# Wider unread streams, and a matrix inverse moved forward by a step, in a fused recurrence and expert kernel

## The chip, the cores and the metric

The kernel runs on one core of a Trainium2 chip. The metric is device time in microseconds from start to end of one launch. The engines are PE (TensorE: matrix products), DVE (VectorE), ACT (ScalarE), POOL (GpSimd) and SP (SyncE, which here does nothing but issue DMAs). Each works through its own instructions in order.

## What is computed

A linear recurrence with a 40x40 state for each of 32 heads (4 batches by 8), over 768 positions, then a layer of eight experts with one chosen for each token, then a dense layer with a squared ReLU.

```python
for t in range(S):                        # 768 positions, batch x heads = 32
    y[:, :, t] = np.einsum('bhd,bhde->bhe', rt, state)
    Sa = np.einsum('bhde,bhe->bhd', state, at)
    state_decay = state * wt[:, :, None, :] - np.einsum('bhd,bhe->bhde', Sa, bt)
    state = state_decay + np.einsum('bhd,bhe->bhde', vt, kt)
...
h = np.maximum(xc[mask] @ w1[e], 0.0)     # 3072 tokens, D 320, F 1024, 8 experts
y[mask] = gate_w[mask, None] * (h @ w2[e])
...
r = np.maximum(x @ w_in, 0.0); return (r * r) @ w_out      # 320 x 2048 x 320
```

## The kernel before

The recurrence is done in 24 **steps** of 32 positions; four steps are a **slab**, so a step is the first, second, third or fourth of its slab (`r = c%4`), and step numbers here count from 0. In a step each head needs the inverse of a 32x32 triangular matrix, which is made for a whole slab at once (128 matrices, one to a partition). The way of those matrices sets the order of much of the work around the change:

1. `L(c)` multiplies a chunk's operands, and its DVE part leaves the triangular table in `zs`; SP stores it to DRAM (`nt<-zs`, L154).
2. `tul(c)` loads it back with heads on partitions into `TU` (`tu<-nt`, L157): four loads a slab. In `run`, the first two are issued at the start of the slab before, the other two right behind their stores (`lst`).
3. `inv(sl)` inverts the two 16x16 halves on DVE: 14 pairs of a product (L177) and a sum (L179). At its end ACT and DVE write the off-diagonal part, transposed, into `TW`, and SP stores both to DRAM (`td<-tu`, `td<-tw`, L187). Before, about three fifths of its pieces come in the third step (places 12 to 32 of that step's table) and the rest in the fourth (places 0 to 8).
4. `ttfill(c,H)` loads one half (`H` 0 or 1, 16 heads each) of a step's matrices into `TT` and `SW` (L213, eight loads of 16 KB). It is issued right behind the stage V of the step before, since V is the last to read `TT`, which exists once.
5. `Pst` (L196) is the first product that reads them; `Qst` (L204) completes the inverse. `Pst` of the next step's half 0 is the last stage of a step (`P0+` in `ORD`).

The order of PE's stages is written out by hand (`ORD`, `ORD2` for third steps, `END`). Between the stages `pump` issues what stands in a table `sched` at places 0 to 32: pieces of the inverse, of decay factors, of routing and of weight conversion. All loads and stores named here share SP's queue, and an issue that must wait holds back what stands behind it.

Stages Z, U and S begin with **unread streams** (`keep`, L94): products whose result nobody reads, written to the unused end of the stage's PSUM bank. They multiply 128 columns of the identity by 256 (Z) or twice by 192 (U and S) bf16 columns of it. The stage V (L260) has none.

```python
ORD=('Z0 U1- V1- Q0 Y0- K1- T0 X U0 V0 S1- K0 R S0 P1 Z1 Y1- T1 Q1 L P0+').split()
```

After the recurrence come the experts and the dense layer (from about 646 us), which the change doesn't touch.

Of the kernel before, what the change touches and what calls it, by code (L numbers as in the profile page):

```python
# [12 lines left out]
BF16 = mybir.dt.bfloat16  # L13
# [7 lines left out]
class Attn:  # L21


    IB=3.4
    I2=(12, 32)
    I3=(0, 8)
    RT=(13, 18)
    RP=(0, 8)
    MP=(12, 26)
# [61 lines left out]
    def pair(s): return s.pp.tile([128,2,512],F32,tag='pp',name='pp')  # L91
    def keep(s,o):

        b=s.ident.bitcast(BF16); s.nc.tensor.matmul(o,b[:,0:128],b[:,0:o.shape[1]],start=True,stop=True)  # L94
    r=0
    def pump(s,n):
        while n>0 and s.fill: s.fill.pop(0)(); n-=1
# [137 lines left out]
            nc.scalar.copy(out=ys[64:128,16*k:16*k+16].rearrange('p (x i r) e -> p x i r e',i=2,r=2)[:,:,i],in_=src)  # L235
    def Zst(s,c,H):
        nc=s.nc; zs=s.g(s.ZS,c); m=s.M1; z=s.Z; pt=s.slot()
        s.keep(pt[:,256:512])
        for j in range(4):
            for i in range(4):  # L240
                h=16*H+4*i+j
                nc.tensor.matmul(pt[32*i:32*i+32,40*j:40*j+40],zs[:,h,:],m[:,h,0:40],start=True,stop=True)
        nc.scalar.activation(out=z[:,4*H:4*H+4,0:40],in_=pt[:,0:160].rearrange('p (g d) -> p g d',d=40),func=AF.Copy,scale=-1.0)
    def Ust(s,c,H):

        nc=s.nc; z=s.Z; tt=s.TT; pt=s.pair()
        for k in range(2): s.keep(pt[:,k,320:512])
        for ii in range(2):
            for j in range(4):
                for k in range(2):  # L250
                    i=2*k+ii; b=slice(64*k,64*k+64); n=160*ii+40*j
                    nc.tensor.matmul(pt[96:128,k,n:n+40],tt[b,4*H+j,32*i:32*i+32],z[b,4*H+j,0:40],start=True,stop=True)  # L252
        for k in range(2):
            nc.scalar.copy(out=s.VU[96:128,16*H:16*H+16].rearrange('p (k x) d -> p k (x d)',k=2)[:,k],in_=pt[96:128,k,0:320])
    def Vst(s,c,H):

        nc=s.nc; z=s.Z; tt=s.TT; ut=s.UT; pt=s.slot()
        for j in range(4):
            g=4*H+j; q=j//2; par=j%2
            nc.tensor.matmul(pt[64*par:64*par+64,128*q:128*q+128],z[:,g,:],tt[:,g,:],start=True,stop=True)  # L260
        nc.scalar.copy(out=ut.rearrange('p (H i q) t -> p H q i t',H=2,i=4)[:,H,:,:,32:64],
                       in_=pt[:,0:256].rearrange('p (q i t) -> p q i t',q=2,i=4))
    def Sst(s,c,H):
        nc=s.nc; ys=s.YS; m=s.VU; mn=s.M1; d=s.g(s.DL,c+1); pt=s.pair()
        for k in range(2): s.keep(pt[:,k,320:512])
        for n in range(8):
            for k in range(2):
                h=16*H+8*k+n
                nc.tensor.matmul(pt[64*k:64*k+40,k,40*n:40*n+40],ys[:,h,:],m[:,h,:],start=True,stop=True)  # L269
        for k in range(2):  # L270
            h=slice(16*H+8*k,16*H+8*k+8)
            nc.vector.tensor_tensor(out=mn[0:40,h,0:40],in0=pt[64*k:64*k+40,k,0:320].rearrange('p (x d) -> p x d',d=40),  # L272
                in1=d[:,h].unsqueeze(2).to_broadcast([40,8,40]),op=ALU.mult)
# [19 lines left out]
    def run(s, sink, more=None, before=None):  # L293
# [26 lines left out]
        for c in range(NC):  # L320
            sl=c//4; r=s.r=c%4; nx=sl+1<s.NS; last=c==NC-1; order=s.END if last else s.ORD2 if r==2 else s.ORD
            if before: before(c)
            sched=[[] for _ in range(NP+1)]
            def add(items,p0,p1):
                for i,f in enumerate(items): sched[p0+i*(p1-p0)//len(items)].append(f)
            def take(budget):
                o=[]
                while s.invq and budget>0: j,f=s.invq.pop(0); o.append(f); budget-=j
                return o
            at=lambda p,*f: sched[p].extend(f)  # L330
            xs=[]; Ls=[]

            if c==0:
                at(6,lambda: (s.tul(4),s.tul(5)),*s.decay(3))
                at(7,lambda: s.prod(6,(V,G,G))); at(9,lambda: s.prod(7,(V,G,G)))
                Ls+=[6,7]
            for P in (sl+1,sl+2):
                d=c-4*(P-2); A=2*P; B=A+1
                if P>=s.NS or P<2: continue
                if d==4: at(0,lambda A=A: (s.tul(2*A),s.tul(2*A+1)))  # L340
                if d==(0 if P>2 else 1): add(s.decay(A),0,14)
                if d==(1 if P>2 else 2): add(s.decay(B),0,12)
                for k in range(4):
                    if d==k+1: at(s.PP,lambda x=2*A+k,w=s.PA[k]: s.prod(x,eng(w)))
                    if d==min(k+2,4): Ls.append(2*A+k)
            if nx:
                if r==2: s.invq=s.inv(sl+1); add(take(s.IB),*s.I2)
                if r==3: add(take(99),*s.I3)
            add(late[0],*s.RP); add(late[1],*s.SC); late=([],[])
            if more:  # L350
                m0,m1=more(c); add(m0,4,NP); add(m1,s.MP[0],s.MP[1])
            if c>1:
                x,pre,post,sc=sink(c-2,s.XT) or ([],[],[],[])
                xs.append(x); add(pre,*((18,22) if last else s.RT)); late=(post,sc)
                if last: add(post+sc,22,30); late=([],[])
            if last:
                x,pre,post,sc=sink(c-1,s.XT) or ([],[],[],[])
                xs.append(x+pre+post+sc)
            pc=[0]
            def pump(n=1):  # L360
                for _ in range(n):
                    if pc[0]<=NP:
                        for f in sched[pc[0]]: f()
                    pc[0]+=1
            def lst(x):
                s.L(x)
                if x<4*sl+8: s.tul(x)
            for st in order:
                k=st[0]; H=int(st[1]) if st[1:] else 0; b=c-st.endswith('-')+st.endswith('+')
                if c==0 and st=='U0': s.turn_tt(); s.L(4); s.L(5); s.Pst(0,0); s.Pst(0,1); s.Qst(0,0); s.Qst(0,1)  # L370
                if b<0: continue
                if k=='Z': s.Zst(b,H); s.load_v(b+1,H)
                elif k=='Y': s.Y(b,H); s.load_y(b+1,H)
                elif k=='T': s.Stt(b,H)
                elif k=='U': s.Ust(b,H)
                elif k=='V':
                    s.Vst(b,H)
                    s.ttfill(b+1,H)
                elif k=='K':
                    s.KBt(b,H)  # L380
                    if H: s.load_k(b+8)
                elif k=='R':
                    hs=[(1,c)] if st=='R1' else [(1,c-1),(0,c)][c==0:]
                    s.RUV([H for H,b in hs])
                    for H,b in hs: s.load_r(b+1,H)
                elif k=='S': s.Sst(b,H); s.load_vu(b+1,H)
                elif k=='P' and b: s.Pst(b,H)
                elif k=='Q' and b: s.Qst(b,H)
                elif k=='X':
                    for f in xs.pop(0) if xs else (): f()  # L390
                elif k=='L':
                    for x in Ls[len(Ls)>1 and c>0:]: lst(x)
                pump(s.PW[k])
                if st=='T0' and c and len(Ls)>1: lst(Ls[0]); pump()
            while pc[0]<=NP: pump()
        x,pre,post,sc=sink(NC-1,s.XT)
# [409 lines left out]
def build(tc, ins, out):  # L806
    nc = tc.nc
    NC = 24
    NPC, NPD = 7, 7
    with ExitStack() as ctx, tc.manual_schedule():  # L810
# [4 lines left out]
        with ExitStack() as c2:  # L815
# [2 lines left out]
            fctx = ctx.enter_context(ExitStack())  # L818
            at = Attn(tc, ins, NC, c2, ident, c3, "right")
            rt = Route(tc, ins, ident, at.ps, cp, dr, at.cp)  # L820
            conv = cv.seq(0, NPC, 2) + cv.seq(NPC, NPD, 1) + cv.seq(NPD, 16, 0)
            NV = {16: 6, 17: 6, 18: 6, 20: 6, 21: 6, 22: 6, 23: 6}

# [60 lines left out]
```

## Time and profile before

| | us |
|---|---|
| median of 3 runs | 1178.79 (1176.95 to 1184.74) |
| profiled execution, its own time | 1181.23 |
| its span, first to last instruction | 1179.5 |
| PE busy with products | 989.7 |
| DVE busy | 610.5 |
| ACT busy | 485.5 |
| POOL busy | 294.2 |

The span is what the trace covers; what lies around it in the profiled execution is 1.7 us. Mean granted TensorE clock over the span: 0.835 of full speed; the clock has two levels, 1.2 GHz (0.50) and 2.4 GHz (1.00), so a mean between them tells how the time is shared out. A busy share is an average over stages with different limits, so it is read by stretch.

### The profile page before, as it was taken

To read this page: it belongs to the slowest core of one execution; us is meant where nothing else is said; L and a number is where in the kernel's file an instruction comes from. 1 tells how busy PE (TensorE), PEld (TensorE's weight loads), DVE (VectorE), ACT (ScalarE), POOL (GpSimd) and SP (SyncE) were. 2 spreads that over 40 slices of the span, in tenths; PEclk is the share of its full clock that TensorE was granted. 3 is DMA by queue.
4 is the path that set the end of the run, shared out by engine and by line. 5 is a ranking of instruction groups with operands and counts; after the bars stand their busy time and mean duration, and the time that the engine had idled before them with its cause. 6 is when DMAs were issued, how large, how long until landed. Compare 5 with 4: busy or idle time off the path is not lost.

```text
span 1179.5 us, 40064 instructions
## 1 busy us (share of the span) xinstructions
PE 989.7 (84%) x17280; PEld 902.3 (77%) x17280; DVE 610.5 (52%) x1132; ACT 485.5 (41%) x1115; POOL 294.2 (25%) x293
## 2 busy tenths in 40 slices
PE   2196877997898988788785789887999999999997
PEld 2175666775777777576575689886999999999997
DVE  8983463455546334452425698784644444444331
ACT  6343443444444355344332555542433333333331
POOL 6222211321311314332424523225211111110000
PEclk9996776677768568676755799998999999999999
DMA  6656555455445444447532898873000010100000
GB/s 186 169 158 192 146 129 147 122 131 144 120 124 139 113 117 124 127 143 188 138 86 80 239 273 257 284 232 109 22 28 28 28 28 27 29 29 24 13 12 20
DMA packets 165306, 138.68 MB, mean 118 GB/s; under 512 B 109887, under 2 KB 139237, under 8 KB 165121
## 3 DMA queue, kind: packets, MB, share of 16 engines
q1 hardware_dynamic: 160865, 124.97, 38.4%
q0 software_dynamic: 4256, 11.06, 3.0%
q8 instruction: 138, 2.26, 0.8%
q14 instruction: 47, 0.39, 0.1%
HBM read 107.65 MB, written 32.85 MB: 119 GB/s over the span
## 4 chain that ended last, share of the span: by engine, by line
PE 62%; DMA 16%; DVE 9%; issue 6%; SPq 5%; ACT 2%; POOL 0%; ACTq 0%; POOLq 0%; DVEq 0%
PE fps L585 18%; PE fps L592 16%; SPq L213 4%; DMA sw<-td 4%; PE pp L252 3%; PE pp L144 3%; PE py L287 3%; PE ps L260 3%; DMA td<-tw 2%; PE ps L436 2%; PE ps L278 2%; PE ps L232 2%; PE pp L269 2%; DMA w<-in_w 2%; PE ps L196 2%
## 5 line engine op out<-in xcount | busy, mean ns | idle before, releaser
L585 PE MATMUL fps<-xl,w1h 128*128 128x256 f32 x768 | 198.8, 286 | 13.3 <-DVE xl L575 13.2
L585 PE MATMUL fps<-xh,w1h 128*128 128x256 f32 x768 | 199.6, 287 | 3.6 <-ACT xh L574 3.6
L585 PEld LDWEIGHTS fps<-xl,w1h 128*128 128x128 f32 x768 | 148.8, 194 | 15.1 <-DVE xl L575 15.1
L592 PE MATMUL fps<-w2h,hh 128*128 128x320 f32 x512 | 158.7, 310 | 0.0
L592 PE MATMUL fps<-w2h,hl 128*128 128x320 f32 x512 | 158.2, 309 | 0.0
L592 PE MATMUL fps<-w2l,hh 128*128 128x320 f32 x512 | 158.1, 309 | 0.0
L585 PEld LDWEIGHTS fps<-xh,w1h 128*128 128x128 f32 x768 | 148.5, 193 | 5.1 <-ACT xh L574 5.1
L693 DVE TENSOR_TENSOR g<-r 128x512 f32<-128x512 f32 x96 | 68.4, 713 | 80.7 <-ACT r L692 80.5
L695 DVE TENSOR_TENSOR hl<-g,hh 128x512 fp32r<-128x512 f32 x96 | 75.3, 784 | 65.9 <-ACT hh L694 65.9
L585 PE MATMUL fps<-xh,w1l 128*128 128x256 f32 x512 | 103.8, 284 | 0.0
L694 ACT CAST hh<-g 128x512 fp32r<-128x512 f32 x96 | 59.6, 621 | 94.2 <-DVE g L693 94.2
L592 PEld LDWEIGHTS fps<-w2l,hh 128*128 128x128 f32 x512 | 96.1, 188 | 0.0
L592 PEld LDWEIGHTS fps<-w2h,hh 128*128 128x128 f32 x512 | 96.1, 188 | 0.0
L592 PEld LDWEIGHTS fps<-w2h,hl 128*128 128x128 f32 x512 | 96.1, 188 | 0.0
L127 POOL TENSOR_TENSOR kb<-kb,qq 104x512 f32<-104x512 f32 x48 | 62.6, 1327 | 123.9 <-DMA kb<-in_kb 45.2
L692 ACT ACTIVATE r<-fps 128x512 f32<-128x512 f32 x96 | 57.0, 594 | 76.4 <-PE fps L585 76.1
L196 PE MATMUL ps<-tt,sw 32*32 32x16 f32 x1536 | 39.7, 199 | 50.9 <-DMA sw<-td 46.3
L585 PEld LDWEIGHTS fps<-xh,w1l 128*128 128x128 f32 x512 | 80.5, 194 | 0.0
L272 DVE TENSOR_TENSOR m<-pp,dl 40x320 f32<-40x320 f32 x92 | 44.8, 487 | 65.5 <-PE pp L269 63.9
L196 PEld LDWEIGHTS ps<-tt,sw 32*32 32x32 f32 x1536 | 31.0, 129 | 61.3 <-issue 32.8
L144 PE MATMUL pp<-a,kb 40*64 40x32 f32 x1536 | 40.3, 267 | 35.6 <-POOL kb L127 29.4
L144 PEld LDWEIGHTS pp<-a,kb 40*64 40x64 f32 x1536 | 37.2, 190 | 37.4 <-POOL kb L127 30.0
(155 smaller groups left out, 1920.0 us busy)
## 6 DMA issues: line engine op xcount, KB each, us to landing
kb<-in_kb SPq DMA_DIRECT2D x24, 416.0 KB
ut<-in_vE SPq DMA_DIRECT2D x48, 208.0 KB
raw<-in_w SPq DMA_DIRECT2D x16, 512.0 KB
raw<-in_w SPq DMA_DIRECT2D x16, 480.0 KB
w<-in_w SPq DMA_DIRECT2D x12, 468.0 KB
a<-in_a SPq DMA_DIRECT2D x24, 208.0 KB
r<-in_r SPq DMA_DIRECT2D x48, 104.0 KB
c<-in_w_out SPq DMA_DIRECT2D x7, 640.0 KB
```

The lines of the kernel that those rows point to most:

```text
L127: e[1+j].tensor_tensor(out=kv,in0=kv,in1=q[:,:,:,1:17],op=ALU.mult)
L144: nc.tensor.matmul(pt[64*hf:64*hf+64,r,32*p:32*p+32],w[k,8*hf+p,:],x[k,8*hf+p,:],start=True,stop=True)
L196: nc.tensor.matmul(pt[b,16*j:16*j+16],s.SW[b,g,:],s.TT[b,g,32*i+16:32*i+32],start=True,stop=True)
L213: s.nc.sync.dma_start(o, s.td[sl][n,u:u+4].rearrange('g (s t) -> s g t',t=32))
L252: nc.tensor.matmul(pt[96:128,k,n:n+40],tt[b,4*H+j,32*i:32*i+32],z[b,4*H+j,0:40],start=True,stop=True)
L272: nc.vector.tensor_tensor(out=mn[0:40,h,0:40],in0=pt[64*k:64*k+40,k,0:320].rearrange('p (x d) -> p x d',d=40), in1=d[:,h].unsqueeze(2).to_ ...
L585: nc.tensor.matmul(pt[:,256*u:256*u+256],a,b,start=i==0,stop=i==len(ops)-1)
L592: nc.tensor.matmul(pt[:,0:320],a,b,start=first and n==0,stop=last and n==23); n+=1
L692: nc.scalar.activation(out=r,in_=v,func=AF.Relu)
L693: V.tensor_tensor(out=g,in0=r,in1=r,op=ALU.mult)
L694: nc.scalar.copy(out=gh[:,2*m2:2*m2+2],in_=g)
L695: V.tensor_tensor(out=gl[:,2*m2:2*m2+2],in0=g,in1=gh[:,2*m2:2*m2+2],op=ALU.subtract)
```

## The change

- `keep` now streams 512 bf16 columns of a constant table of the router (`us`: ones and a triangle of ones) in one product over a whole PSUM bank, which the stage's own products then overwrite. Z has one, U and S have one in place of two of 192, and V, which had none, gets one.
- The whole inverse of a slab is issued in the third step before it (places 0 to 20), and none of it in the fourth.
- The four loads `tul` of a slab are all issued in the second step (place 4, right behind the fill of half 1), no longer right behind the stores in the first.

```diff
--- before.py
+++ after.py
@@ -21,9 +21,7 @@
 class Attn:
 
 
-    IB=3.4
-    I2=(12, 32)
-    I3=(0, 8)
+    I2=(0, 20)
     RT=(13, 18)
     RP=(0, 8)
     MP=(12, 26)
@@ -91,7 +89,7 @@
     def pair(s): return s.pp.tile([128,2,512],F32,tag='pp',name='pp')
     def keep(s,o):
 
-        b=s.ident.bitcast(BF16); s.nc.tensor.matmul(o,b[:,0:128],b[:,0:o.shape[1]],start=True,stop=True)
+        b=s.WK.bitcast(BF16); s.nc.tensor.matmul(o,b[:,0:128],b,start=True,stop=True)
     r=0
     def pump(s,n):
         while n>0 and s.fill: s.fill.pop(0)(); n-=1
@@ -235,7 +233,7 @@
             nc.scalar.copy(out=ys[64:128,16*k:16*k+16].rearrange('p (x i r) e -> p x i r e',i=2,r=2)[:,:,i],in_=src)
     def Zst(s,c,H):
         nc=s.nc; zs=s.g(s.ZS,c); m=s.M1; z=s.Z; pt=s.slot()
-        s.keep(pt[:,256:512])
+        s.keep(pt)
         for j in range(4):
             for i in range(4):
                 h=16*H+4*i+j
@@ -243,8 +241,7 @@
         nc.scalar.activation(out=z[:,4*H:4*H+4,0:40],in_=pt[:,0:160].rearrange('p (g d) -> p g d',d=40),func=AF.Copy,scale=-1.0)
     def Ust(s,c,H):
 
-        nc=s.nc; z=s.Z; tt=s.TT; pt=s.pair()
-        for k in range(2): s.keep(pt[:,k,320:512])
+        nc=s.nc; z=s.Z; tt=s.TT; pt=s.pair(); s.keep(pt[:,0])
         for ii in range(2):
             for j in range(4):
                 for k in range(2):
@@ -254,15 +251,14 @@
             nc.scalar.copy(out=s.VU[96:128,16*H:16*H+16].rearrange('p (k x) d -> p k (x d)',k=2)[:,k],in_=pt[96:128,k,0:320])
     def Vst(s,c,H):
 
-        nc=s.nc; z=s.Z; tt=s.TT; ut=s.UT; pt=s.slot()
+        nc=s.nc; z=s.Z; tt=s.TT; ut=s.UT; pt=s.slot(); s.keep(pt)
         for j in range(4):
             g=4*H+j; q=j//2; par=j%2
             nc.tensor.matmul(pt[64*par:64*par+64,128*q:128*q+128],z[:,g,:],tt[:,g,:],start=True,stop=True)
         nc.scalar.copy(out=ut.rearrange('p (H i q) t -> p H q i t',H=2,i=4)[:,H,:,:,32:64],
                        in_=pt[:,0:256].rearrange('p (q i t) -> p q i t',q=2,i=4))
     def Sst(s,c,H):
-        nc=s.nc; ys=s.YS; m=s.VU; mn=s.M1; d=s.g(s.DL,c+1); pt=s.pair()
-        for k in range(2): s.keep(pt[:,k,320:512])
+        nc=s.nc; ys=s.YS; m=s.VU; mn=s.M1; d=s.g(s.DL,c+1); pt=s.pair(); s.keep(pt[:,0])
         for n in range(8):
             for k in range(2):
                 h=16*H+8*k+n
@@ -331,21 +327,21 @@
             xs=[]; Ls=[]
 
             if c==0:
-                at(6,lambda: (s.tul(4),s.tul(5)),*s.decay(3))
+                at(6,*s.decay(3))
                 at(7,lambda: s.prod(6,(V,G,G))); at(9,lambda: s.prod(7,(V,G,G)))
                 Ls+=[6,7]
+            if c==1: at(4,lambda: [s.tul(x) for x in (4,5,6,7)])
             for P in (sl+1,sl+2):
                 d=c-4*(P-2); A=2*P; B=A+1
                 if P>=s.NS or P<2: continue
-                if d==4: at(0,lambda A=A: (s.tul(2*A),s.tul(2*A+1)))
+                if d==5: at(4,lambda A=A: [s.tul(2*A+k) for k in range(4)])
                 if d==(0 if P>2 else 1): add(s.decay(A),0,14)
                 if d==(1 if P>2 else 2): add(s.decay(B),0,12)
                 for k in range(4):
                     if d==k+1: at(s.PP,lambda x=2*A+k,w=s.PA[k]: s.prod(x,eng(w)))
                     if d==min(k+2,4): Ls.append(2*A+k)
             if nx:
-                if r==2: s.invq=s.inv(sl+1); add(take(s.IB),*s.I2)
-                if r==3: add(take(99),*s.I3)
+                if r==2: add([f for j,f in s.inv(sl+1)],*s.I2)
             add(late[0],*s.RP); add(late[1],*s.SC); late=([],[])
             if more:
                 m0,m1=more(c); add(m0,4,NP); add(m1,s.MP[0],s.MP[1])
@@ -364,7 +360,6 @@
                     pc[0]+=1
             def lst(x):
                 s.L(x)
-                if x<4*sl+8: s.tul(x)
             for st in order:
                 k=st[0]; H=int(st[1]) if st[1:] else 0; b=c-st.endswith('-')+st.endswith('+')
                 if c==0 and st=='U0': s.turn_tt(); s.L(4); s.L(5); s.Pst(0,0); s.Pst(0,1); s.Qst(0,0); s.Qst(0,1)
@@ -818,6 +813,7 @@
             fctx = ctx.enter_context(ExitStack())
             at = Attn(tc, ins, NC, c2, ident, c3, "right")
             rt = Route(tc, ins, ident, at.ps, cp, dr, at.cp)
+            at.WK = rt.us
             conv = cv.seq(0, NPC, 2) + cv.seq(NPC, NPD, 1) + cv.seq(NPD, 16, 0)
             NV = {16: 6, 17: 6, 18: 6, 20: 6, 21: 6, 22: 6, 23: 6}
```

In one step on PE (slab 1), from the end of X to the stage S of half 1; `us` is the router's table, `ident` the identity. Before:

```order
L94 LDWEIGHTS ident
L94 MATMUL pp<-ident 128x192
L94 LDWEIGHTS ident
L94 MATMUL pp<-ident 128x192
L252 MATMUL pp<-z,tt 32x40 x16
L260 MATMUL ps<-tt,z 64x128 x4
L94 LDWEIGHTS ident
L94 MATMUL pp<-ident 128x192
```

After:

```order
L92 LDWEIGHTS us
L92 MATMUL pp<-us 128x512
L249 MATMUL pp<-z,tt 32x40 x16
L92 LDWEIGHTS us
L92 MATMUL ps<-us 128x512
L257 MATMUL ps<-tt,z 64x128 x4
L92 LDWEIGHTS us
L92 MATMUL pp<-us 128x512
```

One stream in place of two stands ahead of U, and a new one ahead of V.

On SP at the change from a first to a second step, the last store of a table, then the fill of half 1 (`tt<-td`, `sw<-td`). Before:

```order
L226 DMA ym<-in_ra 40x512
L154 DMA nt<-zs_115 32x1024
L102 DMA a_93<-in_a 104x512
L157 DMA tu<-nt 32x32x32
L217 DMA m_122<-in_vt 32x16x40
L213 DMA tt<-td 32x4x32
L213 DMA sw<-td 32x4x32
```

After:

```order
L224 DMA ym<-in_ra 40x512
L152 DMA nt<-zs_115 32x1024
L100 DMA a_93<-in_a 104x512
L215 DMA m_122<-in_vt 32x16x40
L211 DMA tt<-td 32x4x32
L211 DMA sw<-td 32x4x32
```

The load `tu<-nt` no longer stands between its store and the fill. It comes later in that second step, ahead of `kb`, `w`, the routing store `xa` and the fill of half 0. After:

```order
L211 DMA tt<-td 32x4x32
L211 DMA sw<-td 32x4x32
L155 DMA tu<-nt 32x32x32 x4
L224 DMA ym<-in_ra 40x512
L102 DMA kb_98<-in_kb 104x1024
L98 DMA w_89<-in_w 104x1152
L459 DMA xa<-xr_203 128x4x320
L211 DMA tt<-td 32x4x32
```

The four loads stand behind the fill of half 1 in place of ahead of it.

On SP in a fourth step, between the fills of half 1 and half 0. Before:

```order
L213 DMA sw<-td 32x4x32
L226 DMA ym<-in_ra 40x512
L104 DMA kb_96<-in_kb 104x1024
L187 DMA td<-tu 128x1024
L187 DMA td<-tw 128x1024
L213 DMA tt<-td 32x4x32
```

After:

```order
L211 DMA sw<-td 32x4x32
L224 DMA ym<-in_ra 40x512
L102 DMA kb_96<-in_kb 104x1024
L211 DMA tt<-td 32x4x32
```

The two stores of the inverse have gone from there; they are issued in the third step.

## Rows read from the trace of the kernel before

**Rows 1.** Busy time by stretch: steps 1 to 22 (us, busy by engine, PEclk, DMA share, GB/s):
```profile
75.80:600.30 524.50, 435.16 (x12161) 360.00 (x12160) 248.45 (x593) 223.98 (x658) 134.34 (x137) 0.71 0.53 140
```

**Rows 2.** Busy time by stretch: steps 10 and 14 (both third) and step 20 (first):
```profile
294.90:316.30 21.40, 20.37 (x578) 16.86 (x578) 10.62 (x34) 9.29 (x30) 9.50 (x10) 0.75 0.50 134
387.30:413.20 25.90, 25.62 (x575) 21.52 (x574) 11.73 (x38) 10.35 (x31) 9.32 (x10) 0.50 0.45 118
...
528.90:546.00 17.10, 16.41 (x507) 13.71 (x506) 5.91 (x12) 9.07 (x29) 8.06 (x7) 0.80 0.56 146
```

**Rows 3.** Waits of PE over the whole trace: total us, times, longest:
```profile
PE ps L196 <- DMA sw<-td: 46.3, 35, 8.7
```

**Rows 4.** The same view of steps 1, 21, then 4, 16, then 3, 19 alone:
```profile
PE ps L196 <- DMA sw<-td: 11.4, 4, 8.7
...
PE ps L196 <- DMA sw<-td: 3.2, 1, 3.2
...
PE ps L196 <- DMA sw<-td: 3.6, 2, 3.2
...
PE ps L196 <- DMA sw<-td: 1.1, 2, 0.6
...
PE ps L196 <- DMA sw<-td: 1.3, 2, 1.1
...
PE ps L196 <- DMA sw<-td: 2.2, 3, 0.8
```

**Rows 5.** Waits of SP's DMA queue over the whole trace:
```profile
SPq L157 <- DMA nt<-zs: 41.5, 17, 4.6
...
SPq L213 <- DMA td<-tu: 19.8, 5, 5.1
```

**Rows 6.** Timeline of SP in step 16, a first step (start us, us):
```profile
447.99 0.31 SPq L154 DMA_DIRECT2D nt<-zs  x1
452.81 0.33 SPq L157 DMA_DIRECT2D tu<-nt  x1
```

**Rows 7.** Timeline of SP in step 15, a fourth step:
```profile
422.73 0.37 SPq L187 DMA_DIRECT2D td<-tw  x1
427.50 0.33 SPq L213 DMA_DIRECT2D tt<-td  x1
```

**Rows 8.** The chain that ended last, in steps 1 and 9 (start us, us):
```profile
79.36 3.98 DMA nt<-zs
...
283.75 8.43 DMA xa<-xr
```

**Rows 9.** Busy time by stretch: one microsecond of step 16 after two table loads were issued:
```profile
443.00:444.00 1.00, 1.00 (x65) 0.96 (x58) 0.02 (x1) 0.95 (x4) 0.00 (x0) 1.00 0.95 141
```

**Rows 10.** Timeline of PE, streams and what follows, four places (start us, us):
```profile
436.01 0.39 PE L94 MATMUL ps<-ident 128*128 128x256 bf16 x1
436.33 0.76 PE L242 MATMUL ps<-m,zs 128*32 128x40 f32 x32
437.03 0.50 PE L94 MATMUL pp<-ident 128*128 128x192 bf16 x2
437.46 1.28 PE L252 MATMUL pp<-z,tt 64*32 64x40 f32 x32
...
444.81 0.33 PE L94 MATMUL pp<-ident 128*128 128x192 bf16 x2
445.07 0.76 PE L252 MATMUL pp<-z,tt 64*32 64x40 f32 x32
...
450.32 0.28 PE L94 MATMUL ps<-ident 128*128 128x256 bf16 x1
450.53 0.49 PE L242 MATMUL ps<-m,zs 128*32 128x40 f32 x30
```

**Rows 11.** Groups of DVE, the two operations of the inverse (count, busy us, mean ns):
```profile
L177 DVE TENSOR_TENSOR tmp<-tu 128x28 f32<-128x28 f32 (+6 forms) x84 | 29.1, 346 | 2.9
...
L179 DVE TENSOR_TENSOR tu<-tu,tmp 128x28 f32<-128x28 f32 (+6 forms) x84 | 22.9, 273 | 2.4
```

## The prediction

> **What bounds the kernel now.** I read the busy times by stretch first. The recurrence, which is all that the change touches, takes 524.5 us for its steps 1 to 22, 23.8 us a step, and PE is busy with products for 435 of them at a mean granted clock of 0.71 [rows 1]. So PE sets the pace, and at 0.71 it has 2.4 GHz for 42% of the time and 1.2 GHz for the rest. What the clock is worth is read from two steps with the same work: step 14 took 25.90 us at 0.50, step 10 took 21.40 us at 0.75 [rows 2]. That is 4.5 us for 0.25, or 1.8 us a step for each 0.1.
>
> Next I read PE's waits. The largest inside the recurrence is the stage P (L196) waiting for a half of the inverse to be loaded: 46.3 us in 35 waits [rows 3]. Split by step kind with the same view: the six second steps wait 11.4 (step 1), 6.0, 6.6, 0.4, 4.5 and 3.2 us (step 21); the first steps 4 to 16 wait 3.6, 0.6, 0.3 and 1.1 us, 5.6 together; the fourth steps 3 to 19 wait 1.3, 1.1, 1.6, 1.1 and 2.2 us, 7.3 together [rows 4] (the first and last of each kind stand there). Third steps hardly wait.
>
> Last I read why the loads are late, in the waits of SP's queue: 41.5 us in 17 waits of a table load (L157) for its own store, 19.8 us in 5 waits of a fill for the stored inverse [rows 5]. In step 16 SP issues the store at 447.99 and then stands until 452.81 before the load goes out; the fill comes behind it [rows 6]. In step 15 the stores of the inverse go out at 422.73, and the first fill that reads them at 427.50 [rows 7].
>
> **Part 1: the table loads move to the second step.** In the first steps nothing then stands between a store and the fills. The load waits for a store that was issued before eight fill DMAs, so it should find it landed. The 5.6 us of the first steps go. So does a part of step 1: the clearing of the expert buffer is queued behind such a load there, whose store took 3.98 us on the chain [rows 8]; I take 3.4 us. The rest of the second steps is another matter. Their last wait is for the fill of half 0, which stands behind a load of keys, one of decay factors and the routing store `xa`; in step 9 the chain runs 8.43 us through `xa` alone [rows 8]. The moved loads join that train ahead of it. One of them fills the DMA engines for about a microsecond (share 0.95 at 141 GB/s, which is its 128 KB) [rows 9], so four put about 4 us in front of a train that starts some 4 us earlier. I therefore count on 4.5 us more from the second steps (step 17, where neither keys nor factors are loaded, and the waits of half 1), 8 in all. The bounds: nothing of steps 5 to 17 and 4 x 1 us lost there for the later loads (8 - 4.5 - 4, about zero), or all their waits (8 + 13 = 21).
>
> **Part 2: the whole inverse in the third step.** Its stores then go out a good ten microseconds before the first fill that reads them, which ends the 7.3 us of the fourth steps: the stores took under 5 us [rows 7]. The price is DVE's order. The inverse costs (29.1 + 22.9) / 6 = 8.7 us a slab [rows 11], of which some 40% now also has to fit into the first 20 places of the third step, ahead of the evacuation of S and ahead of `TW`, for which ACT must wait with the evacuations of P and Z behind it; SP's wait for it holds back only operands of the next step. DVE is busy for 11.73 of 25.90 us in step 14 [rows 2], so 3.5 us more still fit: I take 0. The bound is those 3.5 us, wholly on the path, in five slabs: 17 us.
>
> Waits together: 5.6 + 7.3 + 8 = 21 us gained, from 13 to 34.
>
> **Part 3: the streams.** PE has no slack in steps without waits (25.62 busy of 25.90), so every column is on the path. At 1.2 GHz a stream of 256 takes 0.32 us to the start of the next stage, and two of 192 take 0.43; at 2.4 GHz 0.21 and 0.26 [rows 10]. Each further 128 columns so cost 0.11 or 0.05, and one of 512 should take 0.54 or 0.32. For a half-step Z gains 0.22 (or 0.11), U and S 0.11 each (0.06), V 0.54 (0.32): 0.98 or 0.55, and 1.96 or 1.10 us a step. Over 23 steps that is 45 or 25 us. At the clock forecast below (0.80, so 60% at full speed) it is 1.44 x 23 = 33, of which some 4 us fall into the waits that stay in second steps: 29 us lost.
>
> **Part 4: the clock.** Here no row of before shows the streams of 512, so I bound the gain. Below, none: the streams were there before, at a mean of 0.71. Above, nearly full speed, which the third rival prices. Step 20, at 0.80, is the nearest row [rows 2]: a first step with no table load left to issue, no wait of that kind, and a clock 0.09 above the mean. I take 0.80 for what follows from shorter waits and denser streams together. For 17 steps that is 17 x 1.62 = 27.5 us; in the five second steps whose fill still sets the end I count half, 4. Together 32 us, from 0 to the 83 of the third rival.
>
> PE's own activity speaks for caution. Step 14 shows that being busy isn't enough: 25.62 of 25.90 us busy without a wait, and 0.50 throughout [rows 2]. The Trainium skill (TensorE: Matmul & The Clock Gate, "What's actually happening") says that the default state is throttled and activity releases it, by how busy PE has been; by that, step 14 should have run at full speed and the time would fall as in the third rival. The row differs, and I follow it.
>
> **The sum.** -21 + 29 - 32 = -24 us. The profiled execution took 1181.23 us (its span 1179.5 and 1.7 around it), so it would take 1157; the median of the runs, 1178.79, lies 2.4 us lower, which gives 1155.
>
> **The rivals.** *The streams are only a cost* (ends slower): the clock stays at 0.71, where streams cost 1.60 x 23 - 4 = 33 us, the waits give 21, and the result is +12, 1191; with part of the third step's DVE price, up to 1205. For it: step 14, cold with streams in it and no wait. Against it: step 20. It decides from a rise of the mean clock below (29 - 21) / 32 x 0.09, about 0.02. *The waits stay*: the train of the second steps grows by the four loads and the clock rises by half as much; -13 + 31 - 16 = +2, about 1180. For it: the fills of second steps wait for transfers, not for SP. Against: first and fourth steps wait for SP alone. *Full clock*: with waits and thin stretches gone the recurrence runs near 0.95; 0.24 x 18 x 17 = 73 us and 10 from second steps, with 27 - 4 for the streams: -21 + 23 - 83 = -81, 1098. For it: 42% of the time is at 2.4 GHz already, waits and all. Against: step 14. This is also where the rule of the page above would lead. *The change does nothing* would need the loads to be late for another reason, which rows 6 and 7 exclude.
>
> **How the numbers follow.** Main forecast 45% (1130 to 1167), waits stay 22% (1167 to 1190), streams only a cost 18% (1190 to 1205), full clock 15% (1090 to 1130). A measurement here can tell about 1% from no change, 12 us: below 1167 is faster, above 1191 slower. So faster 0.60, same 0.22, slower 0.18. The range leaves out about half of the full-clock case and a third of the slow one: 1110 to 1195.
>
> **What would show it.** Waits of L196 for `sw` near 25 us, with none over 1 us in first steps 4 to 16 and in fourth steps; SP's wait of the table loads for `nt` near zero; streams of 512 at 0.54 and 0.32 us; mean clock of the recurrence 0.80. It is wrong if the clock stays below 0.74, if DVE holds ACT and PE in third steps, or if the second steps become longer by more than their streams.

## The result, and the profile after

The changed kernel takes 1165.07 us (median of 4 runs, 1163.06 to 1167.9) against 1180.62 for the kernel before (4 runs): a ratio of 0.9869, 95% interval 0.9827 to 0.9911. That is 15.5 us faster; the forecast was 1155, in a range of 1110 to 1195. In every comparison here a run more than 1.5% above the fastest of its kernel is left out; there was one, of e3 (1161.51 us).

Busy time by stretch, changed kernel, steps 1 to 22 [rows 1]:

```profile
78.70:585.70 507.00, 410.51 (x12061) 331.40 (x12120) 242.95 (x592) 223.84 (x658) 133.02 (x137) 0.78 0.57 144
```

The 22 steps take 507.0 us, 17.5 less than before, and the clock is 0.78 in place of 0.71, close to the 0.80 forecast. PE's busy time is read too low here: eight streams a step make 176 in these steps, all 176 weight loads of them are in the trace, but only 116 of the products, so 60 have no record. A missing one leaves a gap of up to 0.47 us at the low clock and 0.25 at the high one; the 60 gaps come to 19 us. So PE was busy for about 429 us, 6 less than before [rows 1], though it had more columns to stream, and the time between products fell from 89 to about 78.

Split by kind of step, the 17.5 us lie in the fourth steps (115.0 us before, 103.4 after, five steps each) and the first (116.2 and 108.7); second steps went from 152.2 to 150.1, and third steps became longer, 118.1 to 121.7. In first and fourth steps the clock rose most, from 0.74 and 0.72 to 0.85.

The same view, steps 10 and 14 (third) and step 20 (first) [rows 2]:

```profile
290.60:317.20 26.60, 24.00 (x575) 19.59 (x578) 13.36 (x44) 11.26 (x32) 9.25 (x10) 0.63 0.55 155
381.00:407.20 26.20, 24.12 (x575) 19.62 (x579) 13.54 (x44) 11.17 (x32) 9.20 (x10) 0.63 0.56 154
513.50:534.00 20.50, 16.47 (x506) 13.46 (x511) 5.60 (x12) 9.23 (x28) 8.03 (x7) 0.83 0.64 169
```

Third steps did not become shorter: step 14 takes 26.20 us at 0.63, where it took 25.90 at 0.50 with fewer columns, and step 10 takes 26.60 at 0.63, where it had taken 21.40 at 0.75. DVE works 1.8 us longer in step 14, and the longest stop of PE there is 0.5 us.

Waits of PE over the whole trace, then of step 1, step 21 and step 19 alone [rows 3, 4], then those of the whole steps 1 to 22:

```profile
PE ps L194 <- DMA sw<-td: 29.7, 21, 5.4
...
PE ps L194 <- DMA sw<-td: 7.7, 6, 5.4
...
PE ps L194 <- DMA sw<-td: 4.5, 2, 3.0
...
PE ps L194 <- DMA sw<-td: 1.6, 1, 1.6
...
PE ps L194 <- DMA sw<-td: 27.8, 19, 5.4
PE ps L194 <- issue: 14.9, 8, 2.8
PE ps L194 <- DMA r<-in_r: 2.6, 1, 2.6
```

The wait for `sw` fell from 46.3 to 29.7, near the 25 forecast. But the last two lines have to be read with it. The stage P now stands for 14.9 us with nothing that the trace names as the cause ("issue"), which was 0.3 us before. The whole steps 1 to 22 before:

```profile
PE ps L196 <- DMA sw<-td: 45.2, 33, 8.7
...
PE ps L196 <- ACT tt L206: 2.2, 2, 1.2
...
PE ps L196 <- issue: 0.3, 1, 0.3
```

All idle time of P in these steps is 45.3 us, against 47.7 before. The wait changed its name more than its length. By kind of step it is 7.0, 27.7, 0.5 and 10.1 us (first to fourth), against 6.6, 33.3, 0.7 and 7.2 before: what went is in the second steps, and nothing went in first and fourth steps, where the prediction took 12.9 us away.

Waits of SP's queue [rows 5]:

```profile
SPq L211 <- PE ps L257: 54.4, 24, 3.8
...
SPq L155 <- DMA nt<-zs: 3.8, 2, 2.4
...
SPq L152 <- DMA td<-tw: 1.2, 3, 0.7
```

SP's two waits are gone as forecast: 41.5 us for `nt` are 3.8, and no fill waits for `td` any more (19.8 before; the 1.2 us are a store's). What stands ahead of the fills now is the first line: they wait until the stage V (L257), the last reader of `TT`, is through. Before, that wait was shorter:

```profile
SPq L213 <- PE ps L260: 34.8, 14, 7.2
```

The stores of the inverse in step 14 go out at 398.62, 17 us ahead of the first fill that reads them, at 415.98 in step 15; before, that fill had to wait for them until 427.50 [rows 7].

```profile
398.62 0.34 SPq L185 DMA_DIRECT2D td<-tu  x1
399.29 0.34 SPq L185 DMA_DIRECT2D td<-tw  x1
...
415.98 0.68 SPq L211 DMA_DIRECT2D tt<-td  x1
```

The chain that ended last still runs through `xa` in second steps, in step 9 for 7.86 us [rows 8]:

```profile
280.00 7.86 DMA xa<-xr
```

Timeline of PE, streams at the low and at the high clock [rows 10]:

```profile
339.88 0.61 PE L92 MATMUL ps<-us 128*128 128x512 bf16 x1
340.42 1.12 PE L257 MATMUL ps<-tt,z 128*64 128x128 f32 x8
...
346.70 0.39 PE L92 MATMUL ps<-us 128*128 128x512 bf16 x1
347.02 0.66 PE L257 MATMUL ps<-tt,z 128*64 128x128 f32 x8
347.61 0.39 PE L92 MATMUL pp<-us 128*128 128x512 bf16 x1
347.93 0.77 PE L265 MATMUL pp<-vu,ys 128*40 128x40 f32 x30
```

From a stream to the stage behind it are 0.54 us, and 0.32 at full speed: the forecast prices, exactly.

The groups of DVE, the two operations of the inverse [rows 11]:

```profile
L175 DVE TENSOR_TENSOR tmp<-tu 128x28 f32<-128x28 f32 (+6 forms) x84 | 26.0, 310 | 4.3 <-DMA tu<-nt 2.5
L177 DVE TENSOR_TENSOR tu<-tu,tmp 128x28 f32<-128x28 f32 (+6 forms) x84 | 25.6, 304 | 2.2
```

The work of the inverse is the same, 51.6 us against 52.0; only its place has changed.

### The profile page after: what moved, and what is told of

Read it like the earlier page. It is cut to its first block, busy times and chain, and to the rows that moved or that the text cites. A ratio compares the mean times of both kernels' runs of the same rounds, so it can differ in the third digit from the quotient of the medians.

```text
span 1164.3 us, 39901 instructions
## 1 busy us (share of the span) xinstructions
PE 965.1 (83%) x17172; PEld 873.4 (75%) x17236; DVE 606.3 (52%) x1132; ACT 485.1 (42%) x1115; POOL 292.5 (25%) x293
## 4 chain that ended last, share of the span: by engine, by line
PE 70%; DVE 10%; DMA 9%; issue 7%; ACT 2%; SPq 1%; POOL 0%; ACTq 0%; POOLq 0%; DVEq 0%
PE fps L580 20%; PE fps L587 16%; PE pp L142 4%; PE pp L249 4%; PE ps L257 3%; PE ps L92 3%; PE py L283 3%; PE pp L265 3%; PE ps L431 3%; PE ps L274 2%; PE ps L240 2%; DMA sw<-td 2%; DMA xa<-xr 2%; PE ps L230 2%; PE ps L194 2%
## 5 line engine op out<-in xcount | busy, mean ns | idle before, releaser
L580 PE MATMUL fps<-xh,w1l 128*128 128x256 f32 x512 | 104.3, 286 | 0.0
L194 PE MATMUL ps<-tt,sw 32*32 32x16 f32 x1536 | 35.4, 195 | 48.4 <-DMA sw<-td 29.7
L142 PE MATMUL pp<-a,kb 40*64 40x32 f32 x1536 | 37.0, 255 | 35.9 <-POOL kb L125 31.2
L194 PEld LDWEIGHTS ps<-tt,sw 32*32 32x32 f32 x1536 | 27.8, 125 | 50.9 <-issue 40.5
L142 PEld LDWEIGHTS pp<-a,kb 40*64 40x64 f32 x1536 | 34.0, 175 | 37.5 <-POOL kb L125 31.7
```

Source lines behind the costliest of these rows:

```text
L142: nc.tensor.matmul(pt[64*hf:64*hf+64,r,32*p:32*p+32],w[k,8*hf+p,:],x[k,8*hf+p,:],start=True,stop=True)
L194: nc.tensor.matmul(pt[b,16*j:16*j+16],s.SW[b,g,:],s.TT[b,g,32*i+16:32*i+32],start=True,stop=True)
L580: nc.tensor.matmul(pt[:,256*u:256*u+256],a,b,start=i==0,stop=i==len(ops)-1)
```

## Experiments

They ran in three groups of four, each group on one chip beside its own runs of the kernel before, whose median was 1166.35 us (e1 to e4), 1161.31 (e5 to e8) and 1182.40 (e9 to e12). Chips differ by up to 2%, so kernels are compared by their ratios within a group. The columns on steps 1 to 22 are from one trace each, and the traced execution is not always a typical one: e6's took 1150.38 us where the median of its runs is 1157.90, and those of e9, e10 and e11 took 10 us more than theirs.

| run | what is in it | ratio (95%) | steps 1-22 us | PE busy | PEclk |
|---|---|---|---|---|---|
| e1 | streams of 512 only | 1.0032 (0.9987-1.0076) | 517.6 | 404.2, some 19 missing | 0.78 |
| e2 | inverse and loads moved | 0.9822 (0.9775-0.9868) | 495.5 | 413.8 | 0.73 |
| e3 | inverse moved only | 0.9817 (0.9760-0.9874) | 494.5 | 402.0 | 0.77 |
| e4 | loads moved only | 0.9949 (0.9896-1.0003) | 510.8 | 418.5 | 0.73 |
| e5 | kernel before | one run | 512.2 | 419.9 | 0.73 |
| e6 | changed kernel | 0.9969 (0.9944-0.9995) | 497.9 | 394.7, some 19 missing | 0.79 |
| e7 | as e2, no streams | 0.9791 (0.9758-0.9824) | 479.8 | 400.9 | 0.71 |
| e8 | as e3, late in the third step | 0.9930 (0.9907-0.9954) | 502.1 | 424.9 | 0.72 |
| e9 | first part of the inverse early | 0.9979 (0.9951-1.0007) | 534.0 | 429.1 | 0.72 |
| e10 | as e2, again | 0.9866 (0.9821-0.9911) | 521.4 | 432.0 | 0.71 |
| e11 | changed, six streams for four | 0.9952 (0.9924-0.9981) | 527.4 | 439.9 | 0.81 |
| e12 | before, no streams | 0.9916 (0.9883-0.9948) | 517.7 | 421.3 | 0.65 |

**e1, the streams alone.** The kernel before with these lines of the change (S has the same as U, and `at.WK = rt.us` is set):

```diff
-        b=s.ident.bitcast(BF16); s.nc.tensor.matmul(o,b[:,0:128],b[:,0:o.shape[1]],start=True,stop=True)
+        b=s.WK.bitcast(BF16); s.nc.tensor.matmul(o,b[:,0:128],b,start=True,stop=True)
...
-        s.keep(pt[:,256:512])
+        s.keep(pt)
...
-        nc=s.nc; z=s.Z; tt=s.TT; pt=s.pair()
-        for k in range(2): s.keep(pt[:,k,320:512])
+        nc=s.nc; z=s.Z; tt=s.TT; pt=s.pair(); s.keep(pt[:,0])
...
-        nc=s.nc; z=s.Z; tt=s.TT; ut=s.UT; pt=s.slot()
+        nc=s.nc; z=s.Z; tt=s.TT; ut=s.UT; pt=s.slot(); s.keep(pt)
```

> The streams of 512 alone, with the loads and the inverse where they were before. Theory A (the schedule gives the gain and the streams are a net cost that they only partly earn back by the clock): 1185 to 1200 us, mean clock of the recurrence 0.72 to 0.75, waits for the inverse as before, about 46 us. Theory B (the streams lift the clock and that gives the gain; the schedule is absorbed): 1160 to 1170, clock 0.77 or more, waits about 46 us.

The ratio is 1.0032, no change that can be told. The clock went up to 0.78 as in the whole change, with none of the waits shortened (51.2 us for `sw`). So the streams raise the clock by themselves (over the whole span and all runs 0.871, against 0.849 for the kernel before beside them), and that paid for them and no more. The new streams also multiply another table than the old (`us` for `ident`); no run separates that from their width.

**e2, the schedule alone.** The two moves, with the old streams, `I2=(0, 20)` and the lines for the first slab as in the whole change; the main lines:

```diff
-                if r==2: s.invq=s.inv(sl+1); add(take(s.IB),*s.I2)
-                if r==3: add(take(99),*s.I3)
+                if r==2: add([f for j,f in s.inv(sl+1)],*s.I2)
...
-                if d==4: at(0,lambda A=A: (s.tul(2*A),s.tul(2*A+1)))
+                if d==5: at(4,lambda A=A: [s.tul(2*A+k) for k in range(4)])
...
-                if x<4*sl+8: s.tul(x)
```

> The moved loads and the moved inverse alone, with the streams of 192 and 256 of before. Theory A: 1140 to 1158 us, below the changed kernel, with waits of P for the inverse near 30 us and a clock of 0.73 to 0.77, since fewer waits let it rise too. Theory B: 1170 to 1180, clock near 0.71.

0.9822, 21 us, at a clock of 0.73 in its trace, no higher than the 0.73 of the kernel before in e5, which ran on another chip. One trace says little here: over the whole span e2's six runs have clocks from 0.848 (the traced one) to 0.868. Their mean is 0.856, that of e3 0.860, against 0.849 beside them; in e10 and e8 it is 0.842 and 0.854, against 0.839 and 0.851. So with the inverse moved the clock is 0.002 to 0.011 higher, with the streams of e1 0.022.

**e3, the inverse alone.** The first three lines of e2's diff, and `I2=(0, 20)`.

> Only the inverse is moved into the third step; streams and table loads as before. By the terms of the prediction the waits of the fourth steps, 7 us, go and the clock gives a few us more: 1165 to 1173. If the order of DVE costs what the bound said (3.5 us a slab), 1178 to 1190.

0.9817, from three runs: within the intervals it gains as much as the whole schedule. Its trace:

```profile
75.80:570.30 494.50, 402.01 (x12161) 334.12 (x12160) 246.16 (x592) 223.93 (x661) 131.13 (x134) 0.77 0.57 146
```

SP's waits tell what the loads add to it; e3 first, then e2:

```profile
SPq L155 <- DMA nt<-zs: 33.0, 15, 4.6
SPq L211 <- PE ps L258: 30.7, 16, 3.4
```

```profile
SPq L211 <- PE ps L258: 42.4, 21, 4.2
...
SPq L155 <- DMA nt<-zs: 3.6, 2, 2.5
```

With the loads moved too, SP is spared 29 us of waiting for `nt`, and waits 12 us longer for the stage V. The fill could not have gone out much sooner, since its buffer was still being read. So the wait for the store was, for the most part, covered by the wait for the buffer.

**e4, the loads alone.** The last three lines of e2's diff, and the lines for the first slab.

> Only the table loads are moved into the second step; streams and inverse as before. By the terms of the prediction 14 us of waits go in first steps, step 1 and second steps, with a few us of clock: 1160 to 1168. If the train of second steps takes the four loads wholly on the path (4 us in each of four second steps), 1175 to 1185.

0.9949, about 6 us, with an interval that just reaches 1, so that no gain at all is not excluded. SP still waits 22.1 us for the inverse.

**e5, the kernel before once more**, for a trace on the chip of e6 to e8.

> The kernel before, unchanged, for a trace of it on the chip of the other experiments, where its runs took 1157 to 1174 us against 1177 to 1185 on the first chip. If the move of the inverse alone gains by shorter work at the same clock, steps 1 to 22 here should take about 518 us at a mean clock near 0.71, 24 us more than in e3_inverse. If what e3_inverse showed was mostly the clock, this trace should show 0.72 to 0.74 here and an idle time of PE that is no longer than the 92 us of e3_inverse. The waits of L196 for sw should be 44 to 50 us by either.

```profile
76.30:588.50 512.20, 419.93 (x12162) 348.10 (x12162) 252.60 (x592) 224.48 (x660) 129.83 (x134) 0.73 0.55 141
```

The same program takes 12 us less for these steps than in [rows 1], at a clock of 0.73. The first chip's trace alone is no measure of what a part gains. Its idle time of PE is 92.3 us, e3's 92.5: what e3's trace has less is busy time at a higher clock (402.0 us at 0.77, for 419.9 at 0.73), though on another chip.

**e6, the changed kernel once more.**

> The changed kernel, unchanged, beside the kernel before on the same chip as the experiments. If the streams of 512 are a net cost on the new schedule, as the ratios 0.9869 (whole change) and 0.9822 (schedule with the old streams) suggest, the ratio is 0.985 to 0.990 here, some 1149 to 1155 us. If they are neutral and those two ratios differ by chance, it is 0.981 to 0.984.

Here it is only 0.3% faster than before, and the intervals of the two measurements (0.9827 to 0.9911, 0.9944 to 0.9995) do not meet. Its waits for `sw` are 43.6 us here and 29.7 on the first chip. Against e5, first and fourth steps are shorter as on the first chip (112.7 for 118.7, 104.3 for 120.4), but third steps are 9.9 us longer (109.8 for 99.9), where they were 3.6 longer there. These are single traces, and that of e6 is of the shortest of its 12 runs.

**e7, the new schedule with no unread stream.** The kernel of e2 with the calls of `keep` left out (the second line stands in U and in S); no result depends on them.

```diff
-        s.keep(pt[:,256:512])
-        for k in range(2): s.keep(pt[:,k,320:512])
```

> The new schedule (loads and inverse moved) with no unread stream at all: the four lines that issue them are left out; the output is unchanged. If a stream is a cost on the path and its clock gives little, this is faster than the schedule with the old streams (0.9822) by the time of the old ones, 0.32 + 2 x 0.43 us a half-step at 1.2 GHz and 1.5 to 2.3 us a step, 35 to 50 us less what the clock loses: ratio 0.95 to 0.975 with a mean clock of steps 1 to 22 of 0.66 to 0.70. If the streams are what holds the clock up, the clock falls to 0.60 or below, 0.12 x 18 us x 23 = 50 us dearer, and the ratio is 0.985 to 1.02.

```profile
76.60:556.40 479.80, 400.90 (x11950) 356.59 (x11943) 246.03 (x593) 223.36 (x657) 128.63 (x135) 0.71 0.60 151
```

The ratio is 0.9791, 1135 us: less than the streams' whole price (0.95 to 0.975) and no loss by the clock (0.985 to 1.02) either. It is the best ratio of all, and 1.8% below the changed kernel on the same chip. (The trace's record of the clock covers only 93% of these steps; in e12 it covers 99%.) Its waits for `sw` are 21.7 us, where e6 has 43.6.

**e8, the inverse late in the third step.** As e3 with `I2=(12, 32)`.

> Of the change only the inverse wholly in the third step, but at places 12 to 32, so that its two stores go out at the end of the third step and not some eight microseconds earlier. If the gain of e3_inverse (0.9817) is that the stores land before the fills read them, part of the fourth steps' wait for sw (7.3 us of before) stays and so does SP's wait of the fill for the store: ratio 0.986 to 0.995. If the gain is that the fourth step no longer holds some 3.5 us of DVE's inverse and ACT's copy at its start, the ratio is 0.980 to 0.984, as in e3_inverse. If the gain is the third step's clock by the place of the work there, the clock of third steps (0.80 in e3_inverse, 0.63 before) falls back below 0.7.

0.9930, short of e3's 0.9817. SP's wait for the stored inverse is gone in e8 as in e3, so that wait and a fourth step free of the inverse, less what they cost in the third step, are worth 0.7% on this chip. That the rest depends on the inverse being early is not shown: e3 ran on another chip, and the changed kernel alone differs by 1.0% between two chips (0.9869 and 0.9969). In the traces e3's lead is in the first steps, 108.6 us at a clock of 0.81, against 118.7 at 0.73 both in e8 and in e5; P's idle time in them is 5.2, 4.7 and 4.7 us, so it is not that wait.

**e9, the first part early, the second left in the fourth step.** The kernel before with one line changed:

```diff
-    I2=(12, 32)
+    I2=(0, 20)
```

> The kernel before with one size changed: the first part of the inverse at places 0 to 20 of the third step instead of 12 to 32; the second part, with the two stores, stays at the start of the fourth step. If the inverse alone gained (0.9817, and 0.993 with the work late in the third step) because its stores go out earlier, nothing is gained here: 0.996 to 1.003. If it gained by where DVE's work lies in the third step, most of the gain is here: 0.983 to 0.99.

0.9979, the interval holds 1. The first part of DVE's work at another place of the third step neither gains nor costs anything that can be told.

**e10, the schedule alone once more**, on the chip of e11 and e12.

> The new schedule with the old streams once more, to stand on the same chip as the next two. The theory that the streams of 512 are a net cost on the new schedule says 0.980 to 0.985 here, with full-speed work of some 305 us in steps 1 to 22 and a clock near 0.72; if the whole change gained 1.3% on one chip and 0.3% on another only because the chips differ, this one is as much nearer to 1 as well: 0.988 to 0.994.

```profile
77.00:598.40 521.40, 432.00 (x12161) 357.55 (x12160) 242.97 (x593) 224.39 (x658) 134.06 (x137) 0.71 0.55 141
```

0.9866, between the two cases.

**e11, six streams in a half-step.** The changed kernel with this at the end of a line of U and of S:

```diff
-...pt=s.pair(); s.keep(pt[:,0])
+...pt=s.pair(); s.keep(pt[:,0]); s.keep(pt[:,1])
```

> The changed kernel with the stream of 512 on both banks of U's and of S's pair, so six streams of 512 in each half-step instead of four: 4 x 0.213 us of full-speed work more a step, 19 us in 22 steps (and 2.2 us a step at half speed). If the clock gives back what streams take (time that PE is at work constant, 409 to 432 us in all runs so far, with the clock in proportion to the work), the ratio stays within 1% of the changed kernel's 0.9969, at a clock of 0.83 to 0.85 in steps 1 to 22. If streams are a cost and no more, it is 19 to 48 us slower: 1.013 or more. If the clock goes to full speed once PE is dense enough, it is faster than the changed kernel: below 0.985 with a clock over 0.9.

```profile
78.70:606.10 527.40, 439.90 (x12209) 322.93 (x12209) 237.82 (x592) 223.67 (x658) 133.10 (x137) 0.81 0.55 139
```

0.9952, which is 0.9% slower than the same schedule with the old streams (e10), and within 1% of e6. The clock rises to 0.81, not to 0.83 and far from full speed.

**e12, the kernel before without streams.**

> The kernel before without its unread streams, on the old schedule; output unchanged. If streams cost a little more than their clock gives back on any schedule, this is 0.3 to 1.2% faster than before (0.988 to 0.997) at a clock near 0.64. If the gain of the schedule without streams (0.9791) needs the new schedule, where fills wait less, this is 0.998 to 1.01.

```profile
75.90:593.60 517.70, 421.29 (x11949) 373.01 (x11949) 248.33 (x593) 224.26 (x657) 131.55 (x137) 0.65 0.55 141
```

0.9916: the old streams cost 0.8% (10 us) as well, although the clock is only 0.65 without them.

## Why the prediction was right, and where its steps were off

**Parts 3 and 4, streams and clock.** The mechanism was right, and so was the balance: +29 and -32 were forecast, a net of -3. e1 measured +4 us on the old schedule, with an interval from -1.5 to +9. The price per stream (0.54 and 0.32 us) and the clock (0.78 for 0.80) were as forecast. What was off is the reason given for the clock: "shorter waits and denser streams together". With the inverse moved the whole span's clock is 0.002 to 0.011 higher (e2, e3, e8, e10), with the streams alone 0.022 (e1). How closely price and clock cancel is best seen from e10 to e11, with one schedule on one chip: 2048 columns more in each half-step would take some 60 us at e10's clock (0.11 or 0.05 us for each 128, 58% of the time at half speed; an estimate). PE's busy time grew from 432.0 to 439.9, by 8. The clock gave back some 85%, and the rest is a loss; by the medians of the runs it is 9 us.

**Rival "streams only a cost".** Its condition, a clock that rises by under 0.02, did not come about, and it was rightly left behind. But there is a comparison that the prediction never made: with no stream at all. There every row stands on the side of cost: 0.8% for the old streams on the old schedule (e12), 1.8% for those of 512 on the new one (e7 against e6).

**Rival "full clock".** Out. Six streams of 512 hold 0.81. The direction of the rule in the Trainium skill (TensorE: Matmul & The Clock Gate, "What's actually happening"), that activity releases the throttle, agrees with the runs: 0.65, 0.71, 0.78, 0.81 with ever more unread columns (e12, e10, e1, e11). That it pays to feed PE for it does not follow, and the runs say no.

**Parts 1 and 2, the waits: -21.** The size came out (21 us in e2, 16 in e10), but by luck in part: its division is wrong, and two errors cancel. The prediction had 13.5 us from the loads (5.6 and 3.4 + 4.5) and 7.3 from the inverse. Measured alone they are 6 and 21, and on top of the inverse the loads add nothing that can be told. The step that failed for the loads is "nothing then stands between a store and the fills": the stage V does, 54.4 us of SP's waits in the changed kernel for 34.8 before. For the inverse, the wait of 7.3 us in fourth steps was taken as the price, with a share of the clock's term. That wait for `sw` did go: no trace of e2, e3 or e10 has any left in fourth steps. But it is not where the 21 us lie: P's idle time in steps 1 to 22 is as long in e3 (47.4 us) as in e5 (42.5), and what is shorter in e3 is PE's busy time, at a higher clock. e8 puts the inverse late in the third step at 0.7% (8 us), close to the 7.3; the other 1.1% was not foreseen. e9, where the first part alone is early, speaks against DVE's place in the third step as its source. Its path stays open, and so does how much of it is the chip, since e3 and e5 to e8 are from different ones.

**The DVE price of zero** was too low, if only by a little. Stage Y in third steps waits for DVE's product (`ym`) where the whole inverse is in the third step; e3 and the kernel before, over steps 1 to 22:

```profile
PE py L285 <- DVE ym L144: 5.5, 4, 2.8
```

```profile
PE py L287 <- DVE ym L146: 1.0, 2, 0.6
```

In third steps alone that wait is 1.4 to 5.5 us in the eight traces with the inverse moved, 1.4 in the changed kernel on the first chip and 3.6 in e6, against 0 to 0.9 in the six others. So DVE does hold PE there, one of the prediction's own signs of being wrong, but for far less than the bound of 17 us, and e3 gains in spite of it.

**The second steps.** "Their last wait is for the fill of half 0", behind `xa`, was right, and it stays: 7.7 and 4.5 us of steps 1 and 21 and 7.86 us of the chain are still there. They did not become longer (152.2 us for the six before, 150.1 after).

**The sign "none over 1 us in first steps 4 to 16 and in fourth steps"** did not come about: step 19 still waits 1.6 us for `sw`, and P's stops in steps 3, 7, 11, 12, 15 and 16 are 1.6 to 2.8 us long under "issue".

**The sum.** Forecast -24, measured -15.5 on the first chip. A clock term that is a little smaller would account for the difference (0.78 for 0.80, 0.02 x 18 x 22 = 8 us by the prediction's own price), but so would the spread between chips: on the chip of e6 the whole change gives 0.3%, some 4 us. Either the streams take back there most of what the schedule gives, or the schedule gives less there. e7's 0.9791 speaks for the first, but the schedule with the old streams was not run on that chip. Whether streams of 512 cost more than the old ones on the new schedule stays open as well: 0.9869 against 0.9822 and 0.9866 on other chips says between nothing and 0.5%.

## What to carry to other kernels

A clock that rises isn't time that is gained: compare the time for which the engine is busy, and always run the version without the filler work. When a wait is taken away in front of a transfer, look what it waits for next, such as the last reader of its buffer; and add up all idle time before the waiting stage, whatever it is put down to, since a wait can change its name and keep its length. Of a change made of several parts, run each alone on one chip: here one part carried the gain, one added nothing on top of it that could be told, and one, the streams, gained nothing.

## What the runs showed of the hardware

**More unread columns, a higher clock.** PE busy time times clock in steps 1 to 22, an estimate of the work in us at full speed, is 274 in e12 (421.29 x 0.65), 307 in e10 (432.00 x 0.71) and 356 in e11 (439.90 x 0.81), all on one chip; e12 has the old schedule. From first to last that is 30% more in 4% more busy time. The columns are not all: e3 has 0.77 and e5 0.73 with the same ones.

**Chips differ in it.** The mean clock of the kernel before over the whole span was 0.849, 0.851 and 0.839 in the three groups, with medians of 1166, 1161 and 1182 us. In the traces the difference lies in third steps: the kernel before takes 118.1 us for its five at 0.66 on the first chip, and 99.9 at 0.79 in e5. With the old streams or none, the four traces from the first chip and that of e9 to e12 have 114.6 to 121.1 us there, the six from the other two chips 99.9 to 105.6. No run shows why.

**Stalls that no semaphore explains.** In step 12 the stage P stops after 28 of 32 products, for 2.78 us, although the products ahead of it read the same loads (timeline of PE, changed kernel):

```profile
355.31 0.49 PE L194 MATMUL ps<-tt,sw 32*32 32x16 f32 x28
358.58 0.24 PE L194 MATMUL ps<-tt,sw 32*32 32x16 f32 x4 [2.78 <-issue]
```

The DMA view of 354 to 359.5 shows one packet of instructions in that stretch:

```profile
q1 hardware_dynamic: 1227, 1.12, 76.8%
q8 instruction: 1, 0.02, 1.0%
```

Of 19 stops of over 0.9 us in steps 1 to 22 that are put down to "issue", 17 have such a packet of 16 KB that landed between a microsecond before the stop and its end; in e5 20 of 20 have one, in e2 21 of 21. There are 96 packets in 507 us, one every 5.3 us, so about half of the stops would have one by chance (an estimate, from stops put at random places of the same stretch). That fits a PE that waits for its own code while other transfers fill the DMA engines, but it is not shown: no run here took the packets away.
